# One PSUM ring for attention, joint transposes of q and k, and no early first-layer groups

## The chip, the cores and the metric

The kernel runs on one core of a Trainium2 chip. The metric is the device time of one execution in microseconds. The engines are named as in the profile: PE (TensorE, matrix products), DVE (VectorE), ACT (ScalarE), POOL (GpSimd) and SP (SyncE, which issues nearly all transfers here). Each works through its own instructions in order.

## The reference

Three layers in a row, all in float32.

```
scores = q k^T / 8 + cum[i] - cum[j], causal         # 4 batches, 8 heads, 576 tokens, 64 wide; cum = cumsum(log f)
x = softmax(scores) v                                # heads side by side: 2304 x 512
h = x w_in ; x2 = max(0.01 h, h) w_out               # first layer: 512 -> 2048 -> 512
expert of each token: greedy by x2 w_gate, 288 tokens per expert, 8 experts
out = max(x2 w1[e], 0) w2[e]                         # second layer: 512 -> 1024 -> 512
```

## The kernel before, in words

**Precision.** Operands of the large products are split into a high and a low part, and a product is made of three (high by high, low by high, high by low).

**Stages.** Attention; the first half of the hidden columns of the first layer (eight column blocks of 128), with the gate's logits; the second half; the second product of the first layer beside the greedy routing; the experts. The change is in attention and in the stage right behind it.

**Attention** goes through 16 pairs of heads. For each pair, `prepare` (L584) loads q and k, transposes them on PE (the operation `flip`, into PSUM), and lets ACT and DVE write the high and low parts of k and q from there; two heads stand in the two halves of the partitions. `offsets` (L674) computes scores with queries on the partitions, in five parts, to get each query's maximum (DVE) and sum of exponentials (ACT); small transposes turn maxima and sums round (`rows` and a second `flip`; the profile names their inputs `xh` and `sm`), and the reciprocals of the sums go out to memory (`invd`) and come back spread over partitions (`R`). `attend` (L771) computes the scores again with keys on the partitions, in four parts named c, a, b and d, takes exponentials (ACT), cuts the triangle on POOL, multiplies by v in two halves of the queries (`values`, the output tile `av`), and scales by the reciprocals (`finish`, DVE, then POOL and a store).

**Order.** The instructions are issued in an order that a planner (`Plan.order`, L119) writes out: each operation has an engine, an estimated duration, operations that it needs, and a rank. An engine that is free takes the ready operation of lowest rank; a rank is no time, and a high rank runs early if nothing else is ready. Pair n has the ranks 12 n plus the constants at the top: ZP for `prepare`, ZO for `offsets`, ZA for `attend`, ZR[1] for the reciprocals; ZW and DW rank the four blocks of weight preparation. An operation that takes a buffer also waits until the buffer taken `depth` takings before in the same ring has been released.

**PSUM in attention** before: eight banks of 512 float32 per partition, as one bank `h` for early groups, two banks `T` for transposes, two double banks `s` for scores, one bank `av`, that is 1 + 2 + 4 + 1.

**Early groups.** The first layer works on nine groups of 256 tokens. NA = 2 of them (L877 to L913) are computed among the attention operations with ranks from ZE upward: 8 column blocks of 12 products each, scaled by ACT and DVE, stored to `gd`. The input of group NA is loaded early too. NE is the number of buffers for early inputs and results; they come from the ring `w`, 40 tiles that weights use as well.

**The stage behind attention** (L923 to L977) starts with weight preparation for w_out (loads named `w`), goes through the groups from NA on, and reloads the results of the groups before NA from `gd` (the tile `ge`) to make their logits. Its PSUM and its SBUF areas reuse those of attention, with waits by tile.

Of the kernel before, what the change touches and what calls it, by code (L numbers as in the profile page):

```python
# [12 lines left out]
FT = mybir.dt.float32  # L13
# [4 lines left out]
OP = mybir.AluOpType  # L18
# [19 lines left out]
ZX = 500  # L38
ZE = 86, 7.5
ZV = -300  # L40
ZP, ZO, ZA, ZH, ZL, ZW, DW = -25.5, -14, 6, 1.5, 2, 65, 16
ZS = 0, 4, 5, 5, 7, 16, 10
ZQ = 3
ZT = -0.5, 7.5
ZR = 6, 18
EB = "h"
NA = 2
NE = 2
LAG = 3
NEAR = 6.5  # L50
NK = 4
TB = 2
PBUF = 4
ZG = 60

# [164 lines left out]
def tile_kernel(ctx, tc, q, k, v, f, w_in, w_out, w_gate, w1, w2, out):  # L220
# [284 lines left out]
    with ExitStack() as c1:  # L505
# [10 lines left out]
        stores = []  # L516
        kept = [wp.tile([128, 512], FT, name="kept", tag="w", bufs=WB) for _ in range(NK)]
        plan.kept = 0
        plan.depth = {"kept": NK, "h": 1, "T": TB, "s": 2, "av": 1, "k": 3, "q": 3, "x3": 4, "x4": 2, "vt": 2, "nm": 2, "sm": 2, "xh": 2, "xi": 2, "xr": 2,
                      "P": PBUF, "R": 2, "xt": 2, "w64": W64[0], "wsq": 1, "wbits": 2, "wst": 2, "w": WB, "wt": 1, "wq": 1, "ex": NE, "eg": NE}  # L520
        plan.chained = dict.fromkeys(("k", "q", "x3", "x4", "vt", "nm", "sm", "kept", "P", "av", "R", "xt", "ex", "eg"))
        op = plan.op

        def mm_ns(*widths):

            return 4 * sum(max(w / 2.4 + 13, 112) for w in widths)


        hd = B * H
        pre = {}  # L530
# [53 lines left out]
        def prepare(n, own, z):  # L584

            b, hp = heads[n]
            h = 2 * hp
            qh, ql, kh, kl, kr = (x[(n + 2) % 3] for x in (QH, QL, KH, KL, KR))
            x3 = {}
            loads, buf = {}, {}  # L590

            def load(j, i):
                src = q if j else k
                if i == 0:
                    x3[j] = at.tile([128, 4, 2, D], FT, name="x3", tag="qk", bufs=4)
                sp.dma_start(x3[j][:, :, i], src[b, h + i, :512].rearrange("(t p) d -> p t d", p=128))

            def load_end(j):
                if j == 0:
                    x3["end"] = at.tile([128, 2, D], FT, name="x4", tag="x4", bufs=2)  # L600
                sp.dma_start(x3["end"][64 * j:64 * j + 64], (q if j else k)[b, h:h + 2, 512:].rearrange("h p d -> p h d"))
            for j in range(2):
                o = op("sp", 450, lambda j=j: load(j, 0), (), z - 8, ["x3"], (), 728)
                buf[j] = o.got
                loads[j] = [o, op("sp", 450, lambda j=j: load(j, 1), [], z - 8, (), buf[j], 728)]
            o = op("sp", 625, lambda: load_end(0), (), z - 8, ["x4"], (), 182)
            buf["end"] = o.got
            loads["end"] = [o, op("sp", 625, lambda: load_end(1), [], z - 8, (), o.got, 182)]
            sets = {}
            outs = {0: [], 1: []}  # L610

            def part(which, z):
                mine = {}

                def flip():
                    mine[0] = p = ps.tile([128, 512], FT, name="T", tag="T", bufs=plan.depth["T"])
                    for t in range(1 if which == "end" else 4):
                        x = x3[which] if which == "end" else x3[which][:, t]
                        pe.transpose(p[:, 128 * t:128 * t + 128], x.rearrange("p s d -> p (s d)"), ident)

                def high(j, c0, w, a):
                    hi = (qh[:, 64:] if j else kh)[:, c0:c0 + w]
                    if j:
                        act.mul(hi, mine[0][:, a:a + w], 0.125)
                    else:
                        act.copy(hi, mine[0][:, a:a + w])

                def low(j, c0, w, a):
                    hi, lo = ((y[:, 64:] if j else y)[:, c0:c0 + w] for y in ((qh, ql) if j else (kh, kl)))
                    vec.scalar_tensor_tensor(lo, mine[0][:, a:a + w], 0.125 if j else 1.0, hi, op0=OP.mult, op1=OP.subtract)  # L630
                end = which == "end"
                o = op("pe", 109 if end else 436, flip, loads[which], z, ["T"] + ([] if end else ["kq"[which]]), buf[which] + (list(sets.values()) if end else []))
                tb = o.got[0]
                if not end:
                    sets[which] = own["kq"[which]] = o.got[1]
                for j, c0, w, a in ([(0, 512, 64, 0), (1, 512, 64, 64)] if end else [(which, 0, 512, 0)]):
                    a_ = op("act", 51 + .833 * w, lambda x=(j, c0, w, a): high(*x), [o], z + ZH, (), [tb, sets[j]])
                    outs[j] += [a_, op("vec", 69 + 1.042 * w, lambda x=(j, c0, w, a): low(*x), [a_], z + ZL, (), [tb, sets[j]])]
            part(0, z)
            part(1, z + ZT[0])  # L640
            part("end", z + ZT[1])
            for u in range(2):
                outs[0].append(op("sp", 450, lambda u=u: sp.dma_start(kr[64 * u:64 * u + 2, :S].bitcast(FT), cumd[:, H * b + h + u]),
                                  [outs[0][0]] + cums + (pads[(n + 2) % 3] if n < 3 else []), z + 1, (), [sets[0]], 30))
            own["ready"] = outs[0] + outs[1] + (pads[(n + 2) % 3] if n < 3 else [])

        def rows(x, dst, need, z, uses, duse):

            mine = {}

            def split(l):
                if l == 0:
                    mine[0] = xh = at.tile([128, 2, 2, 5], FR, name="xh", tag="xh", bufs=2)
                    vec.tensor_copy(xh[:, :, 0], x()[:, :, :5])
                else:
                    vec.tensor_tensor(mine[0][:, :, 1], x()[:, :, :5], mine[0][:, :, 0], op=OP.subtract)

            def flip():
                mine[1] = ps.tile([128, 512], FT, name="T", tag="T", bufs=plan.depth["T"])
                pe.transpose(mine[1][:20, :128], mine[0].rearrange("p u l t -> p (u l t)").bitcast(FT), ident)  # L660

            def copy():
                mine[2] = at.tile([20, 128], FR, name="xr", tag="xr", bufs=2)
                act.copy(mine[2], mine[1][:20, :128])
            o = op("vec", 80, lambda: split(0), need, z, ["xh"], uses)
            xh = o.got[0]
            o = op("vec", 80, lambda: split(1), [o], z, (), uses + [xh])
            o = op("pe", 107, flip, [o], z + 1, ["T"], [xh])
            st = o.got[0]
            o = op("act", 158, copy, [o], z + 2, ["xr"], [st])  # L670
            xr = o.got[0]
            return [op("sp", 450, lambda u=u: sp.dma_start(dst(u).bitcast(FT), mine[2][10 * u:10 * u + 10].bitcast(FT)), [o], z + 3, (), duse + [xr], 30) for u in range(2)]

        def offsets(n, own, z):  # L674
# [9 lines left out]
            def part(ts, z, last):  # L684
# [3 lines left out]
                def product():  # L688
                    if "nm" not in own:
                        tiles()  # L690
                    sc[0] = p = ps.tile([128, 2, 512], FT, name="s", tag="s", bufs=2)
                    for t, i, c0, c1, a in ts:
                        for m, (x, y) in enumerate(((qh, kh), (ql, kh), (qh, kl), (QO, kr))):
                            q = slice(0, 128) if m == 3 else slice(128 * t, 128 * t + 128)
# [38 lines left out]
                    if last:  # L733
                        tots.append(op("act", 280 + .833 * 288, last[u][2], [ms[0]], z + 2, (), [last[u][1], nb, sb]))
                return r
            part([(1, 0, 0, 192, 0), (0, 0, 0, 64, 192)], z, [])
            part([(2, 0, 0, 320, 0)], z + ZQ, [])
            part([(3, 0, 0, 448, 0)], z + 2 * ZQ, [])
            l = part([(4, 0, 0, S // 2, 0)], z + 3 * ZQ, [])
            part([(4, 1, S // 2, S, 0)], z + 4 * ZQ, l)  # L740

# [8 lines left out]
            mine = {}  # L750

            def flip():
                mine[0] = ps.tile([128, 512], FT, name="T", tag="T", bufs=plan.depth["T"])
                pe.transpose(mine[0][:12, :128], own["sm"].rearrange("p u t -> p (u t)"), ident)

            def copy():
                mine[1] = at.tile([12, 128], FT, name="xi", tag="xi", bufs=2)
                act.copy(mine[1], mine[0][:12, :128])
            o = op("pe", 107, flip, [o], z + ZR[1] + 1, ["T"], [sb])
            o = op("act", 158, copy, [o], z + ZR[1] + 2, ["xi"], o.got)  # L760
            o = op("sp", 450, lambda: sp.dma_start(invd[n], mine[1]), [o], z + ZR[1] + 3, (), o.got, 30)

# [8 lines left out]
        def attend(n, own, z):  # L771
# [17 lines left out]
            def score(name, blocks, z):  # L789
# [3 lines left out]

                def product():
                    own["P", name] = at.tile([128, 2, 512], FT, name="P", tag="P", bufs=PBUF)
                    sc[0] = p = ps.tile([128, 2, 512], FT, name="s", tag="s", bufs=2)
                    for n, (i, f0, f1) in enumerate(blocks):
                        for m, (x, y) in enumerate(((kh, qh), (kl, qh), (kh, ql), (kr, qr))):
                            for u in range(2):
# [22 lines left out]
            def values(half, i, z):  # L822
                need, pb, name, a, e, x, y = W[half, i]

                def product():
                    if i == 0:
                        own["av", half] = ps.tile([128, 512], FT, name="av", tag="av", bufs=1)
                    for u in range(2):
                        pe.matmul(own["av", half][64 * u:64 * u + 64, x:y], own["v"][:, i, u], own["P", name][:, u, a:e],
                                  start=i == 0, stop=i == (2, 4)[half])  # L830
                o = op("pe", 4 * (e - a) / 2.4 + 12, product, need + vl + R.get(("av", half), []), z, ["av"] if i == 0 else [],
                       [vb, pb] + R.get(("avb", half), []), form="V")
                if i == 0:
                    R["avb", half] = [o.got[0]]
# [541 lines left out]
```

## Time and profile before

| | |
|---|---|
| median of 3 runs | 977.79 us (976.92 to 982.4) |
| profiled execution | 976.13 us, span 974.4 us |
| PE / DVE / ACT / POOL busy | 96% / 59% / 44% / 45% of the span |
| mean granted PE clock | 0.983 of full speed |
| attention | from the start to about 246 us |
| first half of the first layer | about 246 to 351 us |
| second half | about 351 to 480 us |

Busy time is the time with at least one instruction in work; matmuls overlap, so a mean duration is longer than the distance of two starts, and it is the distance of starts that tells what one costs.

### The profile page before, as it was taken

The numbers are of one execution on the slowest core, as the hardware profiler recorded it, in microseconds if no ns is written. First come the engines' busy times: TensorE is split into PE (matmuls) and PEld (weight loads), VectorE is DVE, ScalarE is ACT, GpSimd is POOL, SyncE is SP. The second block draws the span as 40 slices with busy tenths as digits, with TensorE's granted clock in tenths as the row PEclk, the third lists the DMA queues.
The fourth block names the chain that finished last, engine by engine and source line by source line (L and its number), as shares of the span: only waits on it lengthen the run. The fifth ranks groups of instructions, "written<-read, shape, count | busy, mean of one in ns | idle before, by whom it ended". The sixth has DMA issues, their size and how long they took to land.

```text
span 974.4 us, 21231 instructions
## 1 busy us (share of the span) xinstructions
PE 932.2 (96%) x7923; PEld 805.6 (83%) x7923; DVE 576.5 (59%) x1591; ACT 431.2 (44%) x1077; POOL 440.5 (45%) x568
## 2 busy tenths in 40 slices
PE   6999999999899999999999999999997999999996
PEld 4776778888798998899877777777676999999996
DVE  5788785654578968632535644555563566666641
ACT  5988886776232324422322122222333555555531
POOL 6577783334688848200434443444763112212101
PEclk9999999999899999999999999999997999999998
DMA  5566755533898635531321121121334666557411
GB/s 126 152 179 192 222 160 159 149 122 99 302 368 255 232 124 184 158 86 61 120 65 51 59 65 56 55 65 44 89 128 146 187 193 195 190 191 220 157 60 33
DMA packets 140807, 138.88 MB, mean 143 GB/s; under 512 B 69632, under 2 KB 98816, under 8 KB 140448
## 3 DMA queue, kind: packets, MB, share of 16 engines
q1 hardware_dynamic: 137632, 128.08, 43.2%
q0 software_dynamic: 3072, 9.44, 3.5%
q8 instruction: 62, 1.02, 0.4%
q14 instruction: 41, 0.34, 0.1%
HBM read 106.67 MB, written 30.65 MB: 141 GB/s over the span
## 4 chain that ended last, share of the span: by engine, by line
PE 68%; issue 11%; DVE 10%; DMA 5%; POOL 4%; ACT 1%; SPq 1%; POOLq 0%; DVEq 0%; ACTq 0%
PE acc L1044 20%; PE h L65 18%; PE h L1100 7%; PE y L1113 6%; PE s L65 6%; PE T L65 4%; PE q_ct L1044 3%; DVE kept L65 2%; PE av L65 2%; DMA R<-invd 2%; DVE wbits L65 2%; POOL xt L65 1%; POOL out L1121 1%; DMA X<-xd 1%; SPq L65 1%
## 5 line engine op out<-in xcount | busy, mean ns | idle before, releaser
L65 PE MATMUL h<-X,wh 128*128 128x256 f32 x1728 | 224.4, 286 | 5.7 <-DVE g L65 4.7
L65 PEld LDWEIGHTS h<-X,wh 128*128 128x128 f32 x1728 | 211.3, 191 | 14.0 <-DVE g L65 7.4
L1044 PE MATMUL acc<-wh,gh 128*128 128x512 f32 x576 | 190.4, 404 | 0.0
L447 POOL TENSOR_TENSOR gl<-g,gh 128x512 fp32r<-128x512 f32 x72 | 96.6, 1343 | 111.5 <-ACT gh L446 100.3
L1044 PEld LDWEIGHTS acc<-wh,gh 128*128 128x128 f32 x576 | 109.4, 191 | 20.7
L65 ACT ACTIVATE g<-h 128x256 f32<-128x256 f32 x144 | 55.2, 383 | 156.6 <-PE h L65 153.3
L1044 PE MATMUL acc<-wh,gl 128*128 128x512 f32 x288 | 118.9, 413 | 0.0
L1100 PE MATMUL h<-XE,wh 128*128 128x288 f32 x768 | 118.5, 303 | 0.3 <-ACT XE L1091 0.3
L347 ACT CAST wh<-wst 128x512 fp32r<-128x512 f32 x132 | 79.9, 620 | 82.4 <-DMA wst<-in_moe_w 52.1
L446 ACT CAST gh<-g 128x512 fp32r<-128x512 f32 x72 | 44.5, 621 | 161.8 <-PE acc L1044 131.3
L65 DVE TENSOR_TENSOR wh<-wst,wh 128x512 fp32r<-128x512 f32 x132 | 90.6, 709 | 40.5 <-ACT wh L347 32.0
L1100 PEld LDWEIGHTS h<-XE,wh 128*128 128x128 f32 x768 | 106.6, 191 | 0.6 <-ACT XE L1091 0.6
L65 DVE TENSOR_TENSOR g<-g,h 128x256 f32<-128x256 f32 x144 | 59.9, 416 | 78.3 <-ACT g L65 78.1
L65 ACT ACTIVATE kept<-kept,nm 128x192 f32<-128x192 f32 (+2 forms) x192 | 97.1, 507 | 16.8 <-DVE nm L65 15.7
L1113 PE MATMUL y<-eh,wh 128*128 128x288 f32 x512 | 98.3, 296 | 0.0
L1121 POOL DMA_INDIRECT out<-yo,ids x24 | 24.8, 1034 | 129.2 <-DVE yo L1120 120.0
L1113 PEld LDWEIGHTS y<-eh,wh 128*128 128x128 f32 x512 | 79.5, 188 | 0.2 <-ACT eh L1104 0.2
L65 DVE SCALAR_TENSOR_TENSOR wbits<-w,wbits 128x256 int32<-128x256 int32 x128 | 72.9, 574 | 2.6
L65 DVE CUSTOM_DVE_ANT_0 kept<-s,mask 128x192 f32<-128x192 f32 (+4 forms) x160 | 61.4, 425 | 18.1 <-PE s L65 10.3
L1113 PE MATMUL y<-el,wh 128*128 128x288 f32 x256 | 67.9, 296 | 0.0
L65 ACT ACTIVATE P<-s 128x640 f32<-128x640 f32 (+1 forms) x64 | 53.3, 835 | 26.2 <-PE s L65 24.7
L1044 PEld LDWEIGHTS acc<-wh,gl 128*128 128x128 f32 x288 | 55.1, 191 | 10.9 <-issue 2.0
(197 smaller groups left out, 1613.1 us busy)
## 6 DMA issues: line engine op xcount, KB each, us to landing
wst<-in_moe_w SPq DMA_DIRECT2D x128, 256.0 KB
X<-xd SPq DMA_DIRECT2D x10, 1024.0 KB
gd<-g SPq DMA_DIRECT2D x36, 256.0 KB
g<-gd SPq DMA_DIRECT2D x36, 256.0 KB
w<-in_moe_w_in SPq DMA_DIRECT2D x32, 256.0 KB
w<-in_moe_w_out SPq DMA_DIRECT2D x32, 256.0 KB
xd<-xt SPq DMA_DIRECT2D x16, 320.0 KB
R<-invd SPq DMA_DIRECT2D x32, 144.0 KB
```

The lines of the kernel that those rows point to most:

```text
L65: r = getattr(self.engine, name)(*a, **k)
L347: A.copy(r[u][0], x)
L446: A.copy(gh, g)
L447: G.tensor_tensor(gl, g, gh, op=OP.subtract)
L1044: tc.keep_in_program_order(PE.matmul(*a, **k))
L1100: PE.matmul(h[:, :CAP], w, X[:, c, x, :], start=n == 0, stop=n == 3 * NC - 1)
L1113: PE.matmul(yt[c][:, :CAP], w[:, s], a, start=j == 0 and n == 0, stop=j == NJ - 1 and n == 2)
L1121: sd = G.indirect_dma_start(out=out[:, :], out_offset=bass.IndirectOffsetOnAxis(ap=ids[:, 3 * e + t:3 * e + t + 1], axis=0), in_=y, in_off ...
```

## The change

All PSUM of attention comes from one ring of four double banks (`bank()`): scores, transposes and outputs alike; an operation that needs less uses a part. The transposes of q and k of a pair are one operation, k into the first bank and q into the second. The two parts of `offsets` for queries 128 to 383 share a buffer, and so do those for queries 384 to 511 and the first 64. NA becomes 0: no group is computed among the attention operations, all nine are computed in the stage behind it, and only the input of group 0 is loaded early; the reloads `ge` fall away. NE becomes 1. Ranks change.

```diff
-ZP, ZO, ZA, ZH, ZL, ZW, DW = -25.5, -14, 6, 1.5, 2, 65, 16
-ZS = 0, 4, 5, 5, 7, 16, 10
-ZQ = 3
-ZT = -0.5, 7.5
-ZR = 6, 18
+ZP, ZO, ZA, ZH, ZL, ZW, DW = -30.5, -13, 5, -9, 5, 65, 25
+ZS = -1, 4, 7, 1, 7, 13, 14
+ZQ = 1
+ZT = -0.5, 8.5
+ZR = 5.5, 14
-NA = 2
-NE = 2
+NA = 0
+NE = 1
-NEAR = 6.5
+NEAR = 7.5
-TB = 2
+SB = 4
...
-        plan.depth = {"kept": NK, "h": 1, "T": TB, "s": 2, "av": 1, ...
+        plan.depth = {"kept": NK, "s": SB, ...
...
+        def bank():
+            return ps.tile([128, 2, 512], FT, name="s", tag="s", bufs=SB)
...
-            def part(which, z):
+            def part(end, z):
                 def flip():
-                    mine[0] = p = ps.tile([128, 512], FT, name="T", tag="T", bufs=plan.depth["T"])
-                    for t in range(1 if which == "end" else 4):
-                        x = x3[which] if which == "end" else x3[which][:, t]
-                        pe.transpose(p[:, 128 * t:128 * t + 128], x.rearrange("p s d -> p (s d)"), ident)
+                    mine[0] = p = bank()
+                    if end:
+                        pe.transpose(p[:, 0, :128], x3["end"].rearrange("p s d -> p (s d)"), ident)
+                        return
+                    for j in range(2):
+                        for t in range(4):
+                            pe.transpose(p[:, j, 128 * t:128 * t + 128], x3[j][:, t].rearrange("p s d -> p (s d)"), ident)
...
-            part(0, z)
-            part(1, z + ZT[0])
-            part("end", z + ZT[1])
+            part(False, z)
+            part(True, z + ZT[1])
...
-            part([(1, 0, 0, 192, 0), (0, 0, 0, 64, 192)], z, [])
-            part([(2, 0, 0, 320, 0)], z + ZQ, [])
-            part([(3, 0, 0, 448, 0)], z + 2 * ZQ, [])
+            part([(1, 0, 0, 192, 0), (2, 0, 0, 320, 192)], z, [])
+            part([(3, 0, 0, 448, 0), (0, 0, 0, 64, 448)], z + 2 * ZQ, [])
...
-                        own["av", half] = ps.tile([128, 512], FT, name="av", tag="av", bufs=1)
+                        own["av", half] = bank()[:, 0]
```

## Rows read from the trace of the kernel before

**Rows 1.** Stretches: from:to, length, busy us of PE, PEld, DVE, ACT, POOL; clock; DMA
```profile
28.20:40.45 12.25, 12.22 (x140) 9.58 (x139) 9.05 (x39) 10.72 (x33) 5.33 (x10) 1.00 0.60 151
80.16:93.84 13.68, 12.71 (x141) 9.69 (x139) 11.55 (x40) 12.38 (x37) 11.43 (x16) 1.00 0.73 207
106.90:123.65 16.75, 14.97 (x149) 11.26 (x145) 11.79 (x42) 12.06 (x37) 11.58 (x17) 0.90 0.80 218
123.65:136.45 12.80, 12.80 (x145) 10.04 (x142) 10.65 (x43) 10.89 (x35) 10.85 (x17) 1.00 0.66 176
169.78:184.95 15.17, 15.15 (x165) 12.81 (x163) 9.45 (x37) 11.46 (x36) 5.30 (x10) 1.00 0.43 109
```

**Rows 2.** A stretch, instructions on tile h alone: PE, PEld, DVE, ACT
```profile
106.90:246.00 139.10, 29.09 (x192) 24.62 (x192) 6.68 (x16) 5.92 (x16) 0.99 0.51 145
```

**Rows 3.** Fifteen pairs, instructions on the score tile alone: PE, PEld, DVE, ACT
```profile
28.20:238.80 210.60, 116.14 (x1403) 97.06 (x1401) 68.06 (x170) 50.07 (x61) 0.99 0.58 162
```

**Rows 4.** The same stretch, the transposes' tile T: PE, PEld, DVE, ACT
```profile
28.20:238.80 210.60, 25.11 (x147) 14.77 (x147) 22.74 (x54) 25.31 (x82) 0.99 0.58 162
```

**Rows 5.** The same stretch, the output tile av: PE, PEld, DVE
```profile
28.20:238.80 210.60, 52.53 (x480) 31.20 (x480) 13.65 (x30) 0.99 0.58 162
```

**Rows 6.** Timeline of PE, end of attention: start, duration, line, what
```profile
235.87 0.28 PE L65 MATMUL T<-ident,sm 128*12 128x128 f32 x1
235.90 1.67 PE L65 MATMUL h<-X,wh 128*128 128x256 f32 x12
...
242.87 1.33 PE L65 MATMUL h<-X,wh 128*128 128x256 f32 x9
```

**Rows 7.** Chain of waits behind that flip: start, duration, what
```profile
236.48 2.63 DMA invd<-xi
...
239.70 3.40 DMA R<-invd
...
248.94 5.68 DMA w<-in_moe_w_out
...
256.78 9.00 DMA X<-xd
...
265.92 1.67 PE h L65 x12
```

**Rows 8.** Chain of waits, one first-layer group later in that stage
```profile
311.67 11.46 PE h L65 x96
```

**Rows 9.** Timeline of PE, a switch to transposes and back
```profile
35.82 0.66 PE L65 MATMUL T<-ident,x 128*128 128x128 f32 x4
36.31 0.27 PE L65 MATMUL T<-ident,sm 128*12 128x128 f32 x1
36.55 0.40 PE L65 MATMUL s<-kh,qh 64*128 64x288 f32 x2
36.79 0.29 PE L65 MATMUL s<-kh,ql 64*128 64x288 f32 x2
```

**Rows 10.** Timeline of PE, the first pair
```profile
6.41 1.09 PE L65 MATMUL T<-ident,x 128*128 128x128 f32 x4 [0.24 <-DMA x<-in_q]
...
11.44 0.80 PE L65 MATMUL s<-kr,qo 64*128 64x192 f32 x2 [1.78 <-DMA kr<-cumd]
```

**Rows 11.** Timeline of SP's queue: start, time to issue, what
```profile
103.76 0.97 SPq L65 DMA_DIRECT2D X<-xd  x2
...
111.80 1.15 SPq L65 DMA_DIRECT2D R<-invd  x2
...
254.85 0.43 SPq L65 DMA_DIRECT2D ge<-gd  x1
```

**Rows 12.** Waits from 53.3 to 106.9: us in total, times, longest
```profile
PEld av L65 <- POOL P L65: 4.6, 8, 1.0
...
PE av L65 <- POOL P L65: 2.1, 4, 0.7
```

**Rows 13.** DMA from 246 to 266, in total
```profile
DMA packets 3548, 6.65 MB, mean 333 GB/s; under 512 B 256, under 2 KB 1792, under 8 KB 3319
```

More of the change, by code (lines that the diff above doesn't have):

```diff
@@ L518, in tile_kernel @@
         plan.kept = 0
-        plan.depth = {"kept": NK, "h": 1, "T": TB, "s": 2, "av": 1, "k": 3, "q": 3, "x3": 4, "x4": 2, "vt": 2, "nm": 2, "sm": 2, "xh": 2, "xi": 2, "xr": 2,
+        plan.depth = {"kept": NK, "s": SB, "k": 3, "q": 3, "x3": 4, "x4": 2, "vt": 2, "nm": 2, "sm": 2, "xh": 2, "xi": 2, "xr": 2,
                       "P": PBUF, "R": 2, "xt": 2, "w64": W64[0], "wsq": 1, "wbits": 2, "wst": 2, "w": WB, "wt": 1, "wq": 1, "ex": NE, "eg": NE}
-        plan.chained = dict.fromkeys(("k", "q", "x3", "x4", "vt", "nm", "sm", "kept", "P", "av", "R", "xt", "ex", "eg"))
+        plan.chained = dict.fromkeys(("k", "q", "x3", "x4", "vt", "nm", "sm", "kept", "P", "R", "xt", "ex", "eg"))
         op = plan.op
@@ L621, in high @@
                 def high(j, c0, w, a):
                     hi = (qh[:, 64:] if j else kh)[:, c0:c0 + w]
+                    x = mine[0][:, 0, a:a + w] if end else mine[0][:, j]
                     if j:
-                        act.mul(hi, mine[0][:, a:a + w], 0.125)
+                        act.mul(hi, x, 0.125)
                     else:
-                        act.copy(hi, mine[0][:, a:a + w])
+                        act.copy(hi, x)
                 def low(j, c0, w, a):
                     hi, lo = ((y[:, 64:] if j else y)[:, c0:c0 + w] for y in ((qh, ql) if j else (kh, kl)))
-                    vec.scalar_tensor_tensor(lo, mine[0][:, a:a + w], 0.125 if j else 1.0, hi, op0=OP.mult, op1=OP.subtract)
@@ L631, in part @@
-                end = which == "end"
-                o = op("pe", 109 if end else 436, flip, loads[which], z, ["T"] + ([] if end else ["kq"[which]]), buf[which] + (list(sets.values()) if end else []))
+                    x = mine[0][:, 0, a:a + w] if end else mine[0][:, j]
+                    vec.scalar_tensor_tensor(lo, x, 0.125 if j else 1.0, hi, op0=OP.mult, op1=OP.subtract)
+                if end:
+                    o = op("pe", 109, flip, loads["end"], z, ["s"], buf["end"] + list(sets.values()))
+                else:
+                    o = op("pe", 872, flip, loads[0] + loads[1], z, ["s", "k", "q"], buf[0] + buf[1])
+                    sets[0], sets[1] = own["k"], own["q"] = o.got[1:]
@@ L633, in part @@
                 tb = o.got[0]
-                if not end:
-                    sets[which] = own["kq"[which]] = o.got[1]
-                for j, c0, w, a in ([(0, 512, 64, 0), (1, 512, 64, 64)] if end else [(which, 0, 512, 0)]):
+                for j, c0, w, a in ([(0, 512, 64, 0), (1, 512, 64, 64)] if end else [(0, 0, 512, 0), (1, 0, 512, 0)]):
                     a_ = op("act", 51 + .833 * w, lambda x=(j, c0, w, a): high(*x), [o], z + ZH, (), [tb, sets[j]])
                     outs[j] += [a_, op("vec", 69 + 1.042 * w, lambda x=(j, c0, w, a): low(*x), [a_], z + ZL, (), [tb, sets[j]])]
-            part(0, z)
@@ L658, in flip @@
             def flip():
-                mine[1] = ps.tile([128, 512], FT, name="T", tag="T", bufs=plan.depth["T"])
+                mine[1] = bank()[:, 0]
                 pe.transpose(mine[1][:20, :128], mine[0].rearrange("p u l t -> p (u l t)").bitcast(FT), ident)
@@ L667, in rows @@
             o = op("vec", 80, lambda: split(1), [o], z, (), uses + [xh])
-            o = op("pe", 107, flip, [o], z + 1, ["T"], [xh])
+            o = op("pe", 107, flip, [o], z + 1, ["s"], [xh])
             st = o.got[0]
@@ L690, in product @@
                         tiles()
-                    sc[0] = p = ps.tile([128, 2, 512], FT, name="s", tag="s", bufs=2)
+                    sc[0] = p = bank()
                     for t, i, c0, c1, a in ts:
@@ L752, in flip @@
             def flip():
-                mine[0] = ps.tile([128, 512], FT, name="T", tag="T", bufs=plan.depth["T"])
+                mine[0] = bank()[:, 0]
                 pe.transpose(mine[0][:12, :128], own["sm"].rearrange("p u t -> p (u t)"), ident)
@@ L758, in copy @@
                 act.copy(mine[1], mine[0][:12, :128])
-            o = op("pe", 107, flip, [o], z + ZR[1] + 1, ["T"], [sb])
+            o = op("pe", 107, flip, [o], z + ZR[1] + 1, ["s"], [sb])
             o = op("act", 158, copy, [o], z + ZR[1] + 2, ["xi"], o.got)
@@ L795, in product @@
                     own["P", name] = at.tile([128, 2, 512], FT, name="P", tag="P", bufs=PBUF)
-                    sc[0] = p = ps.tile([128, 2, 512], FT, name="s", tag="s", bufs=2)
+                    sc[0] = p = bank()
                     for n, (i, f0, f1) in enumerate(blocks):
@@ L830, in product @@
                                   start=i == 0, stop=i == (2, 4)[half])
-                o = op("pe", 4 * (e - a) / 2.4 + 12, product, need + vl + R.get(("av", half), []), z, ["av"] if i == 0 else [],
+                o = op("pe", 4 * (e - a) / 2.4 + 12, product, need + vl + R.get(("av", half), []), z, ["s"] if i == 0 else [],
                        [vb, pb] + R.get(("avb", half), []), form="V")
```

## The prediction

> **What bounds the kernel now.** The page first: TensorE (PE) is busy 96% of the span, so a gain has to take work or idle time from PE. Then the busy time by stretch, cut where attention repeats: each of those rows runs from one pair of heads to the next, edge to edge at the start of the last 448-column score product. One pair takes 12.25 us early on, 13.68 us with weight preparation beside it, 16.75 us in one bad pair, 12.80 us with three products of an early group inside, and 15.17 us with 24 of them [rows 1]. PE idles 0.03 us in the first of these, 0.97 us in the second and 1.78 us in the third. So attention is bound by PE once nothing disturbs it, and ScalarE (ACT) stands right behind: 10.72 of 12.25 us. At the end of attention the view changes to the chain of waits: from the last flip of the sums (235.87) it is transfers, not PE, that decide when the second first-layer group behind attention begins, at 265.92 [rows 6, 7]. From there on the first layer is dense PE.
>
> **The change part by part, by the profiled execution** (976.13 us, of which 974.4 us are span; the median of the runs shown is 977.79, 1.7 us more).
>
> *Early groups out of attention.* 192 products stand in attention, with 16 ACT and 16 VectorE (DVE) instructions [rows 2]. A pair with 24 takes 15.17 us and one with three 12.80 [rows 1]: 2.37 / 21 = 0.113 us each. Against the 12.25 us pair it is 2.92 / 24 = 0.122. So the 192 cost 21.7 to 23.4 us; I take 22. But 21 of them (12 at 235.90, 9 at 242.87) run beside the closing chain of transfers [rows 6], which doesn't get shorter without them: 21 x 0.113 = 2.4 us come back as idle time. Gain 19.6 us.
>
> *The same groups behind attention.* A group of 96 products takes 11.46 us there [rows 8], so two cost +22.9 us. Their logits ran there before too, so nothing is added for those. Their eight ACT and eight DVE instructions each go along and lie beside the products; so do their stores. Two 1 MB loads of X come, two 1 MB reloads of stored groups (the `ge` tile) go: equal traffic. If DVE, which also prepares weights there, could not cover them, 8 x 0.42 us a group (6.68 / 16, [rows 2]) would be 6.7 us; the stage is PE-bound and gets longer with the same weight work, so I take 0. Balance of both moves: +3.3 us.
>
> *One PSUM ring.* Write and read times of the three old kinds of buffers over 15 pairs are 116.1 + 68.1 + 50.1 = 234.3 us for scores (two slots of 210.6 us: 56% used), 25.1 + 22.7 + 25.3 = 73.2 for transposes (two slots), 52.5 + 13.7 = 66.2 for outputs (one slot) [rows 3 to 5]. Together 373.6 us on four slots of 15 x 12.4 us = 744: 50%, an estimate without the waits between write and read. The new ring is no fuller than the score ring was, but it turns in order: an output that waits for its reciprocals holds up what comes three buffers later, where before it held up only the next output. PE works in order too, so behind the product that waits for a slot stands everything that PE has left, and ACT and DVE soon after. Price by the nearest rows: nothing (the 12.25 us pair) up to 1.43 us a pair (the 13.68 us one).
>
> *Clock.* In the pair with 1.78 us idle the mean granted clock is 0.90, which is 20% of 16.75 us at 1.2 instead of 2.4 GHz, or 1.7 us lost; with 0.97 us idle it stays at 1.00 [rows 1]. The Trainium skill, "TensorE: Matmul & The Clock Gate", section "A second HAM failure mode: psum-queue depth-cycling", says that cycling through PSUM banks lets PE idle briefly between groups often enough that its clock swings between both levels. By that rule the change, which cycles all banks and takes the filler products out, would pay such a loss again and again; the 13.68 us pair, which cycles two double banks with short gaps at full clock, speaks against it. It is the last rival below.
>
> *Merged operations.* The transposes of k and q become one operation, five offset parts become four. A switch to transposes and back costs, by the five transposes from 35.82 to 36.55 (0.73 us, where four run in 0.49, so 0.12 each), 0.73 - 5 x 0.12 = 0.13, plus the first score product behind, 0.24 instead of about 0.14 us to the next start [rows 9]: some 0.23 us. One score part less saves only the late first product, 0.1. Between 0 (other transposes now stand alone) and 0.33 us a pair; I take 0.2, or 3.0 us over 15 pairs. At the start the joint flip waits for q (6.41) instead of k, but PE waits until 11.44 for other data anyway [rows 10]; cost 0, at most 1.3 us.
>
> *Stalls in the first half.* From 28.20 to 123.65 seven pairs take 95.45 us, less 0.7 for six early products; at 12.25 they would take 85.75: 9.0 us are lost. 3.0 of it is in the 16.75 us pair (against about 13.0 beside it), where SyncE issues the X load of an early group at 103.76 and the read-back of the reciprocals comes only at 111.80 [rows 11]; of three such early loads one stays, so I count these 3.0 as gone. The other 6.0 are mostly outputs waiting for the causal select on GpSimd [rows 12], which shares its queue with weight preparation. The later weight ranks (16 to 25 apart) make weights yield more often, but the planner still fills gaps with them, so a third: 2.0. Sum -5.0, between 0 and -9.0.
>
> *No filler in the second half.* There PE idles 0.02 us in a pair, since early products fill the gaps [rows 1]. Without them ACT needs about 10.7 us of each 12.25. I take +0.4 us for six pairs, +2.4; from 0 to 1.43 x 6 = +8.6.
>
> *End of attention.* In the chain X takes 9.00 us from 256.78 on, with a 1 MB reload issued just ahead at 254.85 [rows 7, 11]; the queues move 333 GB/s there [rows 13], so 1 MB less is 3.1 us less. The flip of the sums moves from two ranks ahead of the pair's first full score to four, which I count as 1.5 us. The 5.68 us transfer of weights in the same chain stays. Sum -4.6, from 0 to -6.5.
>
> Total: +3.3 - 3.0 - 5.0 + 2.4 - 4.6 = -6.9 us: 976.1 becomes 969.2. The profiled execution lies 1.7 us under the median, within the scatter of the three runs; I predict **969 us**.
>
> **The rivals.**
> 1. *A wash* (0.20): the moved products come back one for one and the stalls stay, because it is weight preparation that causes them and its amount is unchanged. +3.3 and half of the end's gain, -2.3: 977. For it: planner and engines are the same. Against: 3.0 us hang on early loads that are gone.
> 2. *Slower, bound by ACT and the in-order ring* (0.17): without filler every pair has gaps like those of 80.16 to 93.84. Free of early products, attention now averages (210.6 - 180 x 0.118) / 15 = 12.62 us a pair (28.20 to 238.80, the short last one included); at 13.2 that is 15 x 0.58 = +8.7, with +3.3 and -4.6 a total of +7.4: 983. It decides from about 12.7 us a pair upwards. For it: ACT's 88% and one long-held output in a ring of four. Against: 12.25 us was reached with a ring of two.
> 3. *All stalls go* (0.11): -9.0 instead of -5.0, no loss of filler, merges worth 0.33 a pair (-5.0): +3.3 - 9.0 - 5.0 - 4.6 = -15.3: 961; with the end at its best, 959. For it: the 12.25 us pair. Against: it ran with half the GpSimd work of its followers.
> 4. *The clock swings* (0.04): 1.7 us in each of 16 pairs, +27, makes some 996. The full clock of all but one of the pairs shown speaks against it.
>
> **How the numbers follow.** My forecast, 962 to 975, gets 0.48. A measurement of this kernel tells about 0.5% from no change: below 972.9 is faster, above 982.7 slower. Faster: 0.40 of the forecast, 0.03 of the wash, all of rival 3: 0.54. Same: 0.08, 0.15 and 0.04 of rival 2: 0.27. Slower: 0.13 of rival 2, 0.02 of the wash, 0.04 of rival 4: 0.19. The range that should hold eight in ten runs from 957 (rival 3 with both bounds) to 984 (rival 2).
>
> **What would show it.** Pairs of 12.1 to 12.5 us throughout attention, at a clock of 1.00; no pair of 16 us; the last attention product some 27 us earlier than 246; the second first-layer group behind attention starting near 236 instead of 266; nine groups of about 12.5 us with logits behind it; and the stages after that shifted by one constant. Wrong would be: pairs of 13 us with PE waiting on a read of the scores or outputs, or a start of the second group that hasn't moved by more than 23 us.

## The result and the profile after

The changed kernel takes 964.25 us (median of 4 runs, 962.55 to 964.78); timed beside it, the kernel before takes 979.4. The ratio is 0.984, with a 95% interval of 0.981 to 0.988, so it is faster by some 15 us. A later comparison of the same two kernels gave 0.985 (0.981 to 0.988). The profiled execution takes 962.55 us, span 960.8.

Where the 13.6 us between the two profiled spans come from, cut at the same events in both:

| stretch | before | after | difference |
|---|---|---|---|
| start to the first pair's last 448-column score product | 28.20 | 27.14 | -1.1 |
| from there to the same product of the last pair | 210.60 | 179.79 | -30.8 |
| to the second first-layer group behind attention | 27.12 | 20.44 | -6.7 |
| to the end of that stage (336.17, before 350.78) | 84.86 | 108.80 | +23.9 |
| second half of the first layer | 128.94 | 128.31 | -0.6 |
| second product, routing, experts | 494.68 | 496.32 | +1.6 |

The stretches of single pairs, which answer to [rows 1], with the same columns:

```profile
27.14:39.48 12.34, 11.54 (x143) 9.96 (x141) 8.79 (x37) 10.39 (x35) 5.39 (x9) 1.00 0.64 161
...
76.00:88.85 12.85, 11.96 (x142) 10.04 (x140) 10.11 (x40) 10.58 (x35) 8.41 (x14) 1.00 0.67 185
...
113.84:128.91 15.07, 12.74 (x141) 10.79 (x140) 10.09 (x44) 12.06 (x38) 8.55 (x14) 0.94 0.74 193
...
165.91:177.30 11.39, 11.33 (x141) 9.84 (x139) 8.43 (x36) 10.46 (x35) 7.55 (x12) 1.00 0.52 141
177.30:188.71 11.41, 11.35 (x142) 9.84 (x139) 8.20 (x36) 10.47 (x35) 5.16 (x10) 1.00 0.35 108
...
27.14:206.93 179.79, 170.92 (x2022) 144.99 (x2020) 139.27 (x540) 155.79 (x495) 125.78 (x190) 0.99 0.61 167
```

The reader is to see two things. The last two full pairs take 11.40 us with PE idle 0.06 us, where the best pair of before took 12.25 with 0.03 us idle: the same products but for one transpose, which that pair lacks, have become denser, though PE counted as busy in both. And the pairs with weight preparation beside them still take 11.7 to 12.9 us, and one of them 15.07.

How the products became denser is in PE's timeline of such a pair (start, duration, what, how many; everything is now written to the tile s, so the kind is told by the inputs: q and k are scores, `ident` is a transpose, `P,vt` the product with v):

```profile
181.55 0.28 PE L65 MATMUL s<-kr,qo 64*128 64x64 f32 x2
181.76 0.28 PE L65 MATMUL s<-ident,xh 128*20 128x128 f32 x1
181.88 1.04 PE L65 MATMUL s<-ident,x 128*128 128x128 f32 x8
182.84 2.94 PE L65 MATMUL s<-P,vt 128*64 128x320 f32 x32
185.71 0.28 PE L65 MATMUL s<-ident,sm 128*12 128x128 f32 x1
186.04 0.30 PE L65 MATMUL s<-ident,x 128*128 128x128 f32 x1
186.34 0.40 PE L65 MATMUL s<-kh,qh 64*128 64x288 f32 x2
```

From 186.34 on only score products follow until the next pair's block of transposes. PE goes once through scores, transposes, all 32 products with v, two transposes, and back. In the written order of attention PE changes its kind of product 71 times; in that of before, 208 times.

The end of attention (PE's timeline, answering to [rows 6]; then the chain of waits, answering to [rows 7, 8]):

```profile
202.85 0.27 PE L65 MATMUL s<-ident,sm 128*12 128x128 f32 x1 [0.59 <-DVE sm L65]
...
206.93 0.37 PE L65 MATMUL s<-qr,kr 64*128 64x448 f32 x2
...
212.58 7.45 PE L65 MATMUL h<-X,wh 128*128 128x256 f32 x60 [0.53 <-DVE R L65]
...
227.37 3.12 PE L65 MATMUL h<-X,wh 128*128 128x256 f32 x24 [0.96 <-DMA X<-xd]
```

```profile
203.63 8.45 PE s L65 x104
...
212.58 6.92 PE h L65 x56
219.50 7.74 DMA X<-xd
...
227.37 3.12 PE h L65 x24
...
284.09 11.59 PE h L65 x96
```

From the last flip of the sums to the issue of X it is 16.65 us instead of 20.91, and the load takes 7.74 instead of 9.00. The way to X has changed too: before, it led through the read-back of the reciprocals and a load of weights [rows 7]; now it leads through PE's own products. The stretch of the table, before and after:

```profile
238.80:265.92 27.12, 23.05 (x185) 20.80 (x181) 12.00 (x28) 7.21 (x15) 15.53 (x22) 0.87 0.79 266
```

```profile
206.93:227.37 20.44, 18.05 (x169) 16.17 (x165) 8.95 (x22) 6.57 (x13) 13.75 (x21) 1.00 0.87 276
```

PE idles 4.07 us in the first and 2.39 us in the second. The granted clock is 0.87 in the first, that is, 26% of the 27.12 us at 1.2 instead of 2.4 GHz, 3.5 us lost; in the second it is 1.00. With 1.4 us for 12 early products these make 6.6 of the 6.7 us, an estimate.

### The profile page after: what moved, and what is told of

Its sections match the earlier page's. It is cut to its first block, busy times and chain, and to the rows that moved or that the text cites. A ratio compares the mean times of both kernels' runs of the same rounds, so it can differ in the third digit from the quotient of the medians.

```text
span 960.8 us, 21226 instructions
## 1 busy us (share of the span) xinstructions
PE 915.5 (95%) x7923; PEld 806.7 (84%) x7923; DVE 571.4 (59%) x1591; ACT 424.9 (44%) x1077; POOL 442.7 (46%) x568
## 4 chain that ended last, share of the span: by engine, by line
PE 66%; issue 10%; DVE 9%; ACT 6%; DMA 4%; POOL 3%; SPq 1%; POOLq 0%; ACTq 0%; DVEq 0%
PE h L65 20%; PE acc L1051 20%; PE h L1107 7%; PE y L1120 6%; PE s L65 4%; ACT kept L65 4%; PE T L65 3%; PE q_ct L1051 3%; DMA w<-in_moe_w_in 2%; DVE kept L65 2%; DVE wbits L65 2%; ACT P L65 1%; POOL out L1128 1%; DMA X<-xd 1%; SPq L65 1%
## 5 line engine op out<-in xcount | busy, mean ns | idle before, releaser
L65 PE MATMUL h<-X,wh 128*128 128x256 f32 x1728 | 216.5, 284 | 5.2 <-DVE g L65 3.0
L65 PEld LDWEIGHTS h<-X,wh 128*128 128x128 f32 x1728 | 207.5, 189 | 12.7 <-DVE g L65 8.7
L65 POOL TENSOR_TENSOR wst<-wsq,wbits 128x256 f32<-128x256 f32 x64 | 50.3, 785 | 43.1 <-DVE wbits L65 39.3
```

Of the source, the lines that this page charges most:

```text
L65: r = getattr(self.engine, name)(*a, **k)
```

## The experiments

Two theories stood at first. S (switches): PE changes its kind of product less often, and the ring is what makes that possible. M (moved work): the early groups cost more inside attention than behind it. The room in the ring and weight preparation came up on the way. A ratio below is to the kernel before, with its 95% interval. Per-pair times are mean lengths from one last 448-column score product to that of a later pair.

**No early groups, nothing else.**

```diff
-NA = 2
-NE = 2
+NA = 0
+NE = 1
```

> Kernel before with NA = 0 and NE = 1 alone; PSUM and ranks as before. Theory S (switches: the gain is PE changing less often between kinds of product, 194 changes in 15 pairs before and 63 after, some 0.12 us each): attention loses its 192 early products (-20 to -23 us) but keeps its 11 changes a pair, and the next stage grows by 23: 975 to 980 us, no difference from before. Theory M (moved work: the early groups cost more inside attention than behind it): 964 to 968 us.

Measured: 980.45 us, ratio 0.9988 (0.9970 to 1.0006): no difference.

```profile
28.61:218.23 189.62, 182.77 (x2030) 140.43 (x2027) 140.46 (x547) 162.92 (x495) 124.59 (x191) 1.00 0.57 158
```

Fifteen pairs take 12.64 us each, at 160 changes of kind in the trace's 15 pairs, some 11 a pair. The stretch is 21 us shorter than [rows 3]'s, and the next stage gives that back. M alone falls.

This run also has the cleanest price of a change. Three late pairs without weight preparation hold exactly the products of the changed kernel's 11.40 us pairs, with no idle time and 11 changes each:

```profile
147.52:159.91 12.39, 12.39 (x142) 9.68 (x139) 8.18 (x35) 10.91 (x35) 5.29 (x10) 1.00 0.57 150
159.91:172.29 12.38, 12.38 (x142) 9.67 (x139) 8.23 (x35) 10.97 (x35) 5.28 (x10) 1.00 0.56 147
```

Against 11.40 us with 4 changes, 0.99 us for 7 changes is 0.14 us each.

**No early groups and the new ranks, on the old PSUM buffers** (the edit above and the Z constants, DW and NEAR of the change).

> Kernel before with NA = 0, NE = 1 and all new ranks, but with the old PSUM buffers, separate transposes and five offset parts. If the ranks alone let PE stay with one kind of product, 5 changes a pair and 965 to 968 us; if it needs the ring of four double banks, 9 or more changes a pair and 972 to 985 us, since two score buffers can't hold a run of eight score parts.

Measured: 1002.28 us, ratio 1.022 (1.018 to 1.026), slower than either expectation. 160 changes of kind in the written order, and a new idle time on PE, here by the waits (who waited for whom, us in total, times, longest):

```profile
PE s L65 <- DVE nm L65: 12.1, 16, 1.7
...
PE s L65 <- ACT P L65: 8.5, 11, 0.9
```

```profile
29.56:229.80 200.24, 175.82 (x1940) 137.46 (x1937) 135.99 (x534) 158.16 (x481) 122.15 (x182) 1.00 0.54 147
```

PE waits for reads of the two score buffers and idles 24.4 us in 14 pairs, at a clock of 1.00. The ranks need the ring.

**The ring with the old ranks** (the changed kernel with the Z constants, DW and NEAR of before).

> Changed kernel with the ranks of before (all Z constants, DW and NEAR), ring, joint transposes and NA = 0 kept. If the ring alone makes the long runs: about 5 changes a pair and 963 to 967 us; if the new ranks are needed as well: 8 to 12 changes a pair and 970 to 978 us.

Measured: 995.09 us, ratio 1.013 (1.009 to 1.017), slower, against both expectations. The changes of kind are few, 68, so the ring alone does bring the long runs. But PE stands still behind outputs that hold their places (stretch of 14 pairs; a wait):

```profile
28.16:227.22 199.06, 172.26 (x1939) 149.29 (x1938) 131.68 (x535) 154.16 (x480) 120.63 (x182) 0.94 0.54 147
```

```profile
PE s L65 <- DVE R L65: 11.0, 9, 2.1
```

14.2 us a pair, PE idle for 26.8 us, 11.0 of them by this wait, at a mean clock of 0.94. `DVE R` is the scaling of an output by its reciprocals. This is the mechanism of the prediction's slower rival, an output that holds a place of the ring; the new ranks mostly keep it away. They bring the reciprocals earlier (ZR[1] lies 9 ranks behind ZA instead of 12), but which of the ranks does it was not separated.

**The early groups back, in the ring.**

```diff
-NA = 0
-NE = 1
-EB = "h"
+NA = 2
+NE = 2
+EB = "s"
-                        m["h"] = ps.tile([128, 512], FT, name=EB, tag=EB, bufs=plan.depth[EB])
+                        m["h"] = bank()[:, 0]
```

> Changed kernel with two early groups back inside attention (NA = 2, NE = 2), their product taking a double bank of the ring. Theory S: the products cost what they cost behind attention, plus some 25 more changes of PE and places in the ring, minus what they hide at the end of attention: 962 to 970 us. Theory M: the gain is lost, 974 to 980 us.

Measured: 988.13 us, ratio 1.007 (1.005 to 1.009), slower than both expectations. The trace shows a cause that neither theory had named, two single waits:

```profile
PE s L65 <- DMA X<-xd: 11.3, 1, 11.3
...
PE s L65 <- POOL wh L65: 5.1, 1, 5.1
```

The planner had placed the first early products before their inputs were there, and PE works in order. So the same again with later ranks for them (`ZE = 112, 5` for `86, 7.5`) and earlier weights (`DW = 16`):

> Changed kernel with two early groups back in the ring (NA = 2, NE = 2) as in the run before, where PE waited 11.3 us once for the load of X and 5.1 us for weights, but with their ranks from 112 on instead of 86 and weight ranks 16 apart, so that both are there. Theory S: the two waits go and the early groups cost what they cost behind attention: 962 to 972 us. Theory M (early products in the ring spoil the pairs beside them): 978 us or more.

Measured: 979.58 us, ratio 0.9992 (0.9978 to 1.0006), a time that theory M named. The trace doesn't show M's mechanism, though: one wait for X is left, and the next five pairs behind it have next to no idle time (PE's timeline):

```profile
155.52 1.62 PE L65 MATMUL s<-X,wh 128*128 128x256 f32 x6 [6.97 <-DMA X<-xd]
```

```profile
174.48 0.36 PE L65 MATMUL s<-qr,kr 64*128 64x448 f32 x2
...
179.84 1.67 PE L65 MATMUL s<-X,wh 128*128 128x256 f32 x12
...
184.44 1.68 PE L65 MATMUL s<-X,wh 128*128 128x256 f32 x12
...
188.41 0.36 PE L65 MATMUL s<-qr,kr 64*128 64x448 f32 x2
```

A pair with 24 early products takes 13.93 us, 2.53 more than the changed kernel's 11.40, or 0.105 us a product; behind attention it is 11.59 / 96 = 0.121. So the products spoil nothing in the pairs that hold them. What comes with them is a wait for their input and a mean clock of 0.90 from 140 to 210. Whether an order without that wait would be as fast as the changed kernel wasn't tried.

**No grouping by kind** (`NEAR = 0`).

> Changed kernel with NEAR = 0: the planner no longer prefers to stay with PE's kind of product; in the written order PE changes kind 219 times in attention instead of 71. Theory S (a change costs about 0.12 us): pairs of 12.2 us or more where the changed kernel has 11.4, 10 to 18 us slower, 974 to 982 us. Theory R (the ring with its place for eight banks of anything, not the grouping, makes PE dense): within 4 us of the changed kernel, 960 to 968 us.

Measured: 1010.93 us, ratio 1.031 (1.029 to 1.034): the direction of S, and far more than its price.

```profile
28.91:242.11 213.20, 189.54 (x1929) 139.49 (x1925) 133.61 (x537) 156.24 (x482) 120.91 (x181) 0.95 0.50 136
```

These are 14 pairs of 15.23 us; the changed kernel's first 14 take 171.65 us. PE idles for 23.7 us, 15.9 more than in those, and at a mean clock of 0.95 a tenth of the time runs at 1.2 GHz, which loses 10.7 us (1.7 in the changed kernel, at 0.99). So the run shows that the grouping is needed, but idle time and clock are mixed in. Taken off, they leave 16.6 of the 41.5 us for 140 more changes of kind in the trace, some 0.12 us each: an estimate that agrees with the 0.14 above, here with the ring in place.

**A ring of three** (`SB = 3`).

> Changed kernel with SB = 3, two of the eight banks unused; the written order keeps its 70 changes of kind. If the long runs of score parts live on four buffers: PE waits for reads of scores and outputs in every pair, 0.7 to 2 us a pair, 975 to 995 us. If three are enough: within 4 us of the changed kernel.

Measured: 993.28 us, ratio 1.013 (1.010 to 1.017), with 70 changes of kind. PE waits for the exponentials' reads:

```profile
PE s L65 <- ACT P L65: 10.7, 13, 1.4
```

**One more place per pair: k and q flipped apart.**

```diff
-                o = op("pe", 872, flip, loads[0] + loads[1], z, ["s", "k", "q"], buf[0] + buf[1])
+                o = op("pe", 436, flip, loads[0], z, ["s", "k"], buf[0])
+                o1 = op("pe", 436, flip1, loads[1], z - 0.5, ["s", "q"], buf[1])
```

> Changed kernel with the transposes of k and of q as two operations again, each with a double bank of the ring; the written order changes kind 91 times instead of 71. Theory S: 20 changes of 0.12 us, 2 to 3 us, and one more place taken per pair: 1 to 3 us more if the ring has room, 967 to 970 us; if the ring is full, 975 us or more.

Measured: 1004.6 us, ratio 1.023 (1.020 to 1.027): 39 us above the changed kernel of the same comparison (965.21).

```profile
28.00:240.00 212.00, 183.90 (x1967) 151.33 (x1969) 133.40 (x542) 157.38 (x493) 120.33 (x183) 0.92 0.51 137
```

```profile
PE s L65 <- POOL P L65: 10.1, 11, 2.3
```

PE's longest wait in total is for the causal cut of the exponentials on POOL, not for a place of the ring, and PE's order no longer repeats from pair to pair (3 to 8 changes). So not all of the 39 us is the price of the place: the planner made another order of it.

**One more place per pair: five offset parts** (the `part` calls of before in the changed kernel).

> Changed kernel with the five offset parts of before in place of four; still 71 changes of kind, but one more place in the ring per pair. If only changes of kind count: within 3 us of the changed kernel. If room in the ring counts: PE waits for reads, 970 us or more.

Measured: 978.39 us, ratio 0.997 (0.995 to 0.999): 13 us above the changed kernel, with the same 71 changes of kind. PE waits for exponentials (5.8 us in 13 waits) in place of few long waits for outputs. An undisturbed pair:

```profile
178.34:190.41 12.07, 11.64 (x143) 9.68 (x140) 8.49 (x36) 10.47 (x35) 5.16 (x10) 1.00 0.49 128
```

It takes 0.67 us more than the changed kernel's, with the same four changes and the same ACT time, and PE idles 0.43 us in it instead of 0.06. The changed kernel beside these:

> The changed kernel once more, as the measure for the three beside it: 960 to 967 us.

Measured: 965.21 us. A pair of the changed kernel takes 14 places of the ring; both variants take 15. The ring has no room for a fifteenth without PE waiting, as the five parts show best, although its slots are in use only half of the time by the prediction's estimate. On this evidence the joint transposes and the joined parts save a place more than PE time.

**Weight preparation behind attention** (the loads of the first layer's weights wait for the last store of attention).

> Changed kernel in which the weight preparation of the first layer waits for the last store of attention; it is all done, but behind attention, so the whole gets slower. Looked at are the pairs: if weight preparation is what makes the first nine pairs 12.3 to 12.9 us against 11.4 in the last ones, all pairs take 11.3 to 11.7; if it is the order itself or the early load of X, the first ones stay above 12 us.

Measured in a single execution: 1006.71 us in all, since PE then waits for weights. The early pairs (PE's timeline):

```profile
63.06 0.37 PE L65 MATMUL s<-qr,kr 64*128 64x448 f32 x2
...
74.46 0.37 PE L65 MATMUL s<-qr,kr 64*128 64x448 f32 x2
...
85.86 0.37 PE L65 MATMUL s<-qr,kr 64*128 64x448 f32 x2
```

11.40 us each, the same as the changed kernel's last pairs; later ones take up to 12.09. So weight preparation costs the first nine or ten pairs about 1 us each and the long pair 3.7: from 27.14 to 154.33 ten pairs take 127.2 us, 13.2 more than ten times 11.40.

**The early load of X later.** The long pair of the changed kernel shows how such a loss comes about (DVE's timeline, then PE's):

```profile
124.94 0.29 DVE L65 TENSOR_SCALAR wbits<-w 128x256 int32<-128x256 int32 x1 [1.92 <-DMA w<-in_moe_w_in]
...
126.29 0.41 DVE L65 TENSOR_TENSOR R<-s,R 128x256 f32<-128x256 f32 x1
```

```profile
126.76 0.44 PE L65 MATMUL s<-qh,kh 64*128 64x320 f32 x2 [2.08 <-DVE R L65]
```

A load of weights takes 4.76 us (from 120.77); DVE waits for it with the scaling of an output queued behind; that output holds a place of the ring; PE waits 2.08 us for the place. The X load is issued beside it, at 121.18, so it was moved:

```diff
-stores[:H * (1 + parts(g)[-1][2])]
+stores[:26]
```

> Changed kernel whose one early load of X waits for the stores of the 13th pair instead of the fourth, so that it no longer runs beside weight preparation. If the 15.07 us pair of the changed kernel comes from a weight load that this load delays (DVE waits for it, and the output's read behind it holds a place of the ring), that pair shrinks to 12.3 to 12.9: 2 to 3 us faster, 960 to 963 us. If the pair is long for another reason: no difference.

Measured: 961.04 us, ratio 0.981 (0.977 to 0.985): 4.2 us under the changed kernel of the same comparison by the medians, but the two intervals overlap, so a gain isn't settled. The mechanism moved rather than went: that pair is short now, and another became long, from 77.41 to 92.34.

```profile
89.99 0.63 PE L65 MATMUL s<-qh,kh 64*128 64x320 f32 x2 [1.74 <-DVE R L65]
...
92.34 0.58 PE L65 MATMUL s<-qr,kr 64*128 64x448 f32 x2
```

PE waits there for the same scaling, with no X load near it; in the chain of waits stands a weight load of 4.38 us, from 83.51. So the X load isn't needed for such a pair; the chains of both runs lead to the weight load. This version is the fastest that was run.

## Why the prediction was right in direction and range, and short in size

The prediction had 969 us, 957 to 984; its own case, 962 to 975, holds the measured 964.25. It forecast 6.9 us between profiled executions; 13.6 came.

- *Early groups out and behind* (+3.3): right. Alone, with the end of attention, they change nothing (0.9988). A group behind attention took 11.59 us where 11.46 was counted, and the whole stage grew by 23.9 us where 22.9 was.
- *Merged operations* (-3.0, 0.2 us a pair): this is the term that was mis-sized. It is 0.99 us in an undisturbed pair, 11.40 against 12.39 without early groups, or some 15 us over 15 pairs. The prediction priced the one switch to transposes and back that the joint flip saves by itself. It did not see that four interchangeable double banks let eight score parts and all products with v run in one go, so that of 11 changes of kind in such a pair 4 are left, at 0.14 us each. The row that tells the price, [rows 9], was read: some 0.23 us for a switch there and back, two changes. It was counted once a pair instead of three to four times.
- *Stalls in the first half* (-5.0): wrong. The prediction blamed early X loads and weight ranks; the loss grew. Against their own undisturbed pairs, the nine pairs that have weight preparation beside them without early groups and with the old buffers lose 7.4 us (118.91 from 28.61 to 147.52), the ten of the changed kernel, where it lasts a pair longer, 13.2, and only without weight preparation does that go. This eats part of the 15 us: over 15 pairs 189.62 becomes 179.79, 9.8 us.
- *No filler in the second half* (+2.4): wrong. Undisturbed pairs idle 0.06 us without early products, so the term is about nothing; its error, 2.4 us, goes the other way.
- *End of attention* (-4.6): near in size, not in mechanism. -6.7 came in that stretch, of which 12 early products of before (after its last 448-column product) are 1.4. The load of X became 1.3 us shorter, not 3.1, and the transfer of weights, which was to stay in the chain, is no longer in it; what counted was less idle time and the clock.
- *One PSUM ring* (0 to 1.43 us a pair, taken as nothing): right for this kernel, and for a reason that was not the one given. "No fuller than the score ring was" suggested room; with one place more, five parts cost 13 us.
- *The wash* did not come, but its reason was right: the stalls stayed because weight preparation causes them.
- *The slower rival* did not come, but its mechanism is real: it is the 15.07 us pair, and with the old ranks it is the largest of PE's waits in a kernel 1.3% slower than before. *The clock* rival did not come either (0.99 over the pairs), but the clock fell in some of the variants that stall.

That the total fell inside the range is in part luck: the term that was too small, by some 12 us, and the stalls, which were to shrink by 5.0 and grew by some 6, stand against each other. Of the signs that the prediction named, pairs of 12.1 to 12.5 us throughout did not come; the second group behind attention started 38.6 us earlier, where 30 was expected. And its lower bound of 957 doesn't follow from its terms: rival 3 with the end at its best makes 959.

## What to carry to other kernels

When PE counts as 99% busy, count how often it changes its kind of product and price one change from the timeline, before taking its busy time for work. A shared in-order ring can be half empty on average and still have no room: count the places that each round takes, since one more can cost most of what the whole change gains (13 of 15 us here). A part of such a change tried alone may lose (here the ranks without the ring do, and the ring without the ranks), so test it with the others in place, by taking one out.

## What the runs showed of the hardware

A change of PE between kinds of product (scores, transposes, products with v) costs 0.14 us by undisturbed pairs and some 0.12 us by the run without grouping, an estimate; PE counts as busy meanwhile.

The granted clock falls in several variants whose PE stands still often in attention: 0.94 with the old ranks (26.8 us idle, longest wait 2.1 us), 0.95 without grouping (23.7 us, 3.2 us), 0.92 with k and q flipped apart (28.1 us, 2.5 us), against 0.99 in the changed kernel. At 0.92 over 212 us, 16% of the time ran at 1.2 instead of 2.4 GHz, and 17 us were lost on top of the waits. The rule of the Trainium skill that the prediction weighed ("TensorE: Matmul & The Clock Gate", "A second HAM failure mode: psum-queue depth-cycling") tells of such swings where PE cycles through PSUM banks and idles briefly between groups of products. These variants agree with it; the new ranks on the old buffers, whose PE idled 24.4 us in 14 pairs at 1.00 (longest wait 1.7 us), do not, and neither does the changed kernel, which cycles the same banks. So idle time in total doesn't tell whether the clock falls, and what exactly brings it down was not separated.

The last stages took 1.6 us more with the same instructions, 496.32 us at a mean clock of 0.97 where the kernel before took 494.68 at 0.98. With the later X load they take 494.33, again at 0.98, which is 2 us of that version's gain. The clock moves the way of these differences; why it differs there stays open.
